# Batch 0 of a fused Fourier mixing and ELU block: mirrored rows read forward and turned by flip products, loads and products by rows, and one list of operations

## The chip, the cores and the metric

The kernel runs on one core of a Trainium2 chip. The metric is the device time of one execution in microseconds (us). Three executions of the kernel before took 1909.07, 1910.53 and 1910.87 us; their median is 1910.53. A further execution was taken with the hardware profiler.

## What is computed

The reference takes x of shape (8, 3008, 256) in float32, applies a Fourier transform along the sequence and one along the channels, keeps the real part, and passes every row through two matrix products with an ELU between them:

```python
X = np.fft.fft(x, axis=1)
X = np.fft.fft(X, axis=2)
x = X.real.astype(np.float32).reshape(8 * 3008, 256)
h = x @ w_in                                   # (256, 2048)
g = np.where(h > 0.0, h, np.exp(np.minimum(h, 0.0)) - 1.0)
return (g @ w_out).astype(np.float32)          # (2048, 256)
```

w_in and w_out arrive as float64. The kernel takes them as pairs of 32-bit words and converts them itself.

## The kernel before

**The transform by mirrors.** The real part of a two-dimensional transform of real data needs only sums and differences of mirrored entries. The kernel folds the sequence twice and the channels once, so that a batch becomes small stationary matrices, which are multiplied with cosine and sine matrices. Four tiles xl0 to xl3 (L[0] to L[3]) hold the rows of a batch: L[0] the rows from 0 upward, L[1] those from the end of the batch downward, L[3] those from the middle (HALF = 1504) upward, L[2] those from the middle downward. Each has 128 partitions and six rows (m = 0 to 5) of 256 channels in the free dimension: four rows from the first 512, two from the next 256. Partition p holds rows 4p to 4p+3 of the one part and 2p, 2p+1 of the other. In the mirrored tiles the same partition must hold the mirrored rows, so partition p needs rows further back as p grows. The function load_x gets these (back, L248) by gathers on GpSimd's queue with a table of row numbers; the other two tiles come by plain loads (ahead, L262) on SyncE's queue (SP).

**Folds of batch 0.** fold_x (L683) makes of each tile a sum e and a difference o of mirrored channels, 128x768 each, and then sums and differences of the four e and the four o: the stationaries EO for the real part (e) and the imaginary part (o), of even and odd frequencies. All of it is on VectorE. fold_first (L894) does the same for channel 128 alone, which feeds a transform of its own ("x").

**Transforms.** A Dft (L952) multiplies its six stationary blocks (one for each m) with slices of MC, a matrix of 128x1887 per kind (R, I for real and imaginary, even and odd frequencies; O and J are the odd ones). dft_parts (L909) says which: the products with m = 1, 3, 5 ("odd") go to one PSUM bank, those with m = 0, 2, 4 ("even") to another. copy, unfold ("sum"), plus ("up") and minus ("down") make of the two banks the columns of a ring of 2048 columns in SBUF: Rr for the real, Ir for the imaginary part, and Rb for channel 128.

**Weights.** w_in and w_out come in eight chunks each (Chunk, L367; w0 to w7 and u0 to u7 in the list of names). A chunk is loaded raw (512 KB), and then converted by integer steps on VectorE (top, mantissa, sign: letters a, b, s), ScalarE (power, low, high: p, l, d) and GpSimd (round, multiply, pair: R, M, P). The w_in chunks are folded too: fold_chunk (f) multiplies a chunk with CC on TensorE into a PSUM bank, put_half (Ws, Wc) copies it into Wsc on ScalarE. The last row of Ws has to stand as a column in wex: for chunks 0 and 1 turn_last_row (wm, L651) does it by tiny products with "pick" on TensorE and put_last_row (wex, L662) copies them; for chunks 2 to 7 spread_last_row (L639) writes it to DRAM and reads it back by two DMAs.

**The second stage.** The columns of the ring are taken 256 at a time. A step is one w_in chunk of one such tile: P (mm_P, L1322) and Q (mm_Q, L1327) make h in a bank "H"; V (even_part, L1331) adds channel 128 on VectorE between them; h_minus, below (b), exp (x) and g follow on VectorE and ScalarE; Xa and Xb (mm_plain) multiply with w_out in the first two tiles, and mm_X1 to mm_X3 in all later ones. These first two tiles go in turns, so slot 0 is chunk 0 of tile 0 and slot 1 is chunk 0 of tile 1. A step of a later tile takes 4.8 us, which is PERIOD (T in the code).

**The order.** Everything is put into a list of events with a time, and emitted in the order of these times; operations wrapped in pin keep this order on their engine, so each engine works through a queue that is written out by hand. The DMA loads are not wrapped. FRONT (L1747) is the part of the list for batch 0 and the first slots, written as lines of names with a time. Loads that the front needs are issued ahead of it (L1643 to L1651) or by load_rest (L1670), which waits for the gathers by way of a one-element copy into MC (L1673). In front of all that stand 46 products of zeros on TensorE (L1640), which write a bank that nobody reads. Later batches (1 by mirror_folds on GpSimd, 2 to 7 by quarters) have other code and are not touched.

Of the kernel before, what the change touches and what calls it, by code (L numbers as in the profile page):

```python
# [36 lines left out]
BS = 4  # L37

# [135 lines left out]

@with_exitstack
def kernel(
# [16 lines left out]
    CC_dr = nc.inline_tensor(_chan_consts(), name="chan_mats")  # L193
    PK_dr = nc.inline_tensor(_pick_consts(), name="pick_mats")
# [46 lines left out]
    def load_x(b):  # L241

        L = [
            spool.tile([128, 6 * ND], FP, tag=f"xl{j}", bufs=1, name=f"xl{j}")
            for j in range(4)
        ]

        def back(j, few):  # L248
            cols = slice(0, 2 * ND) if few else slice(2 * ND, 6 * ND)
            c = 1 if few else 0  # L250
            pin(
                nc.gpsimd.indirect_dma_start(
                    out=L[j][:, cols],
                    out_offset=None,
                    in_=xflat,
                    in_offset=bass.IndirectOffsetOnAxis(
                        ap=ix[:, c : c + 1].bitcast(U32), axis=0
                    ),
                    element_offset=(b * SEQ + (HALF if j == 1 else 0)) * ND,
                )  # L260
            )
        def ahead(j, row):  # L262
            nc.sync.dma_start(out=L[j][:, 0 : 4 * ND], in_=xrows(b, row, 4, 128, 4))
            nc.sync.dma_start(
                out=L[j][:, 4 * ND :], in_=xrows(b, row + 512, 2, 128, 2)
            )

        loads = [lambda n=n: back(2 - n // 2, n % 2) for n in range(4)]
        return L, loads + [lambda: ahead(3, HALF), lambda: ahead(0, 0)]
# [278 lines left out]
    def load_mats(ri, kodd, cuts=()):  # L548
        n = (2 * ri + kodd) * BW
        ends = (0, *cuts, BW)  # L550
        for a, z in zip(ends, ends[1:]):
            nc.sync.dma_start(
                out=MC[ri, kodd][:, a:z], in_=MC_dr.ap()[:, n + a : n + z]
            )
# [128 lines left out]
    def fold_x(L, engine_of, cuts_of):  # L683

        ops = {}

        def op(key, o, a, b, f):
            tt = lambda o, a, b, f: pin(
                engine_of(key).tensor_tensor(out=o, in0=a, in1=b, op=f)  # L689
            )  # L690
            cuts = cuts_of(key, o.shape[1])
            for i in range(len(cuts) - 1):
                c = slice(cuts[i], cuts[i + 1])
                ops[key, i] = lambda c=c: tt(o[:, c], a[:, c], b[:, c], f)

        E, O = [], []
        for j in range(4):
            e = spool.tile([128, 6 * 128], FP, tag=f"e{j}", bufs=1, name=f"e{j}")
            o = spool.tile([128, 6 * 128], FP, tag=f"o{j}", bufs=1, name=f"o{j}")
            ev, ov = (  # L700
                t.rearrange("p (m o d) -> p m o d", o=2, d=64) for t in (e, o)
            )
            src = L[j].rearrange("p (m d) -> p m d", d=ND)
            if j in (1, 2):
                src = src[:, ::-1]

            lo, hi = (
                t.rearrange("p m (d o) -> p m o d", o=2)
                for t in (src[:, :, 1:129], src[:, :, 255:127:-1])
            )  # L710
            op(f"e{j}", ev, lo[:, :, ::-1], hi[:, :, ::-1], ALU.add)
            ops[f"c{j}", 0] = lambda e=ev[:, :, 0, 63:64], s=src[:, :, 0:1], j=j: (
                act(e, s)
                if engine_of("c") is nc.vector and j != 1
                else pin(engine_of("c").tensor_copy(out=e, in_=s))
            )
            op(f"o{j}", ov, lo, hi, ALU.subtract)
            E.append(e)
            O.append(o)
        ops["x1", 0] = lambda: act(L[1][0:1, 5 * ND :], L[0][0:1, 0:ND])  # L720
        op("E0", E[0], E[0], E[1], ALU.add)
        op("E2", E[2], E[2], E[3], ALU.add)
        op("EO0", E[1], E[0], E[2], ALU.add)
        op("EO1", E[3], E[0], E[2], ALU.subtract)
        op("O0", O[0], O[0], O[1], ALU.subtract)
        op("O2", O[2], O[2], O[3], ALU.subtract)
        op("EO2", O[1], O[0], O[2], ALU.subtract)
        op("EO3", O[3], O[0], O[2], ALU.add)
        return [E[1], E[3], O[1], O[3]], ops
# [164 lines left out]
    def fold_first(L):  # L894

        c = [t.rearrange("p (m d) -> p m d", d=ND)[:, :, 128:129] for t in L]
        c[1], c[2] = c[1][:, ::-1], c[2][:, ::-1]
        a = spool.tile([128, 6], FP, tag="xa", bufs=1, name="xa")
        g = spool.tile([128, 6], FP, tag="xg", bufs=1, name="xg")
        vtt(a.unsqueeze(2), c[0], c[1], ALU.add)  # L900
        vtt(g.unsqueeze(2), c[2], c[3], ALU.add)
        d = state["x_odd"] = spool.tile([128, 6], FP, tag="xd", bufs=1, name="xd")
        vtt(d, a, g, ALU.subtract)
        e = spool.tile([128, 6], FP, tag="xe0", bufs=1, name="xe0")
        vtt(e, a, g, ALU.add)
        return e


# [9 lines left out]
    def dft_mms(ps, ri, kodd, par, stat, width):  # L918
        for j, (m, c, n, o) in enumerate(dft_parts(ri, kodd, par)):
            mm(  # L920
# [31 lines left out]
    class Dft:  # L952
# [7 lines left out]
        def mms(self, par, ps):  # L960
            dft_mms(ps, self.ri, self.kodd, par, self.stat, 1 if self.first else 128)
# [678 lines left out]
    for _ in range(46):  # L1640
        mm(idle, zero, zero[:, 0:1].to_broadcast([128, 512]), True)
    exp_neg(warm)
    L_first, loads = load_x(0)  # L1643
    for load in loads[:5]:
        load()
    w1_chunks[0].load()
    loads[5]()
    nc.sync.dma_start(out=CC, in_=CC_dr.ap())
    load_mats(0, 0, (BE,))
    w1_chunks[1].load()  # L1650
    nc.sync.dma_start(out=pick, in_=PK_dr.ap())  # L1651
    EO, ops = fold_x(
        L_first,
        lambda key: nc.vector,
        lambda key, n: (0, 4, n) if key in ("e0", "e2") else (0, n),
    )

    def dft_now(d, par, tag):
        d.mms(par, bank(tag))

    R_even, I_even = Dft(0, 0, 0, EO[0]), Dft(1, 0, 0, EO[2])
    R_odd, I_odd = Dft(0, 0, 1, EO[1]), Dft(1, 0, 1, EO[3])
# [7 lines left out]
    def load_rest():  # L1670

        ops["x1", 0]()
        act(MC[1, 0][0:1, 0:1], L_first[1][0:1, 0:1])  # L1673
        load_mats(1, 0)
        w2_chunks[0].load()
        w1_chunks[2].load()
        load_mats(0, 1)
        for chunk in (w1_chunks[3], w2_chunks[1], w1_chunks[4], w2_chunks[2]):
            chunk.load()
        load_mats(1, 1)  # L1680
        w1_chunks[5].load()
        w2_chunks[5].load()

    def open_x(b):
        state["L"], state["loads"] = load_x(b)

    def begin_x_even():
        state["x_even"] = Dft(0, 0, 0, fold_first(L_first), ring=Rb, first=True)

    def copy_row(cols):  # L1690
# [9 lines left out]
        ("xs", begin_x_even),  # L1700
        ("xl1", load_rest),
# [4 lines left out]
    for (key, i) in list(ops):  # L1706
        names[key + "ab"[i] if key in ("e0", "e2") else key] = ops[key, i]
    for c in range(6):
        for name, chunk in ((f"w{c}", w1_chunks[c]), (f"u{c}", w2_chunks[c])):
            for key, fn in zip(  # L1710
                "abpldRsMP",
                (chunk.top, chunk.mantissa, chunk.power, chunk.low, chunk.high,
# [7 lines left out]
        names[f"wex{c}"] = lambda c=c: put_last_row(c)  # L1720
    for k, d, tags in (
        ("x", lambda: state["x_even"], ("pC", "pD")),
        ("R", lambda: R_even, ("pA", "pB")),
        ("I", lambda: I_even, ("pC", "M")),
        ("O", lambda: R_odd, ("pA", "pB")),
        ("J", lambda: I_odd, ("H", "H")),
    ):
        names[f"{k}-even"] = lambda d=d, tags=tags: dft_now(d(), 0, tags[0])
        names[f"{k}-odd"] = lambda d=d, tags=tags: dft_now(d(), 1, tags[1])
        names[f"{k}-copy"] = lambda d=d: d().copy()  # L1730
        names[f"{k}-sum"] = lambda d=d: d().unfold()
        names[f"{k}-up"] = lambda d=d: d().plus()
        names[f"{k}-down"] = lambda d=d: d().minus()
    names["L"] = lambda: [open_x(1)] + [state["loads"][n]() for n in (4, 5)]
    for n in range(4):
        names[f"L{n}"] = lambda n=n: state["loads"][n]()
    for slot in range(8):
# [9 lines left out]
    FRONT = (  # L1747
        (-20.84, "e3 o3"),
        (-19.11, "w0a w0b w0p w0R c3"),
        (-17.62, "w0s w0M"),  # L1750
        (-16.21, "e0a e2b o2"),
        (-14.32, "e2a o0 c2"),
        (-12.89, "E2 f0 O2"),
        (-11.63, "xl1 xs e1 x-even"),
        (-9.8, "e0b c1 o1 c0 x-odd x-copy Wc0"),
        (-8.58, "E0 Ws0 EO0"),
        (-7.29, "wm0 wex0 O0 R-odd"),
        (-5.76, "w1b EO2"),
        (-4.55, "w2b R-even u0b w2d u0a EO1 w1d"),
        (-3.25, "I-odd R-copy w1l w1a x-sum u0l"),  # L1760
# [348 lines left out]
```

## Time and profile before

| | |
|---|---|
| runs | 1909.07, 1910.53, 1910.87 us; median 1910.53 |
| profiled execution | 1909.52 us |
| its span, first to last instruction | 1907.7 us |
| granted TensorE clock over the span | 1.00 |
| TensorE busy | 1899.9 us |
| VectorE, GpSimd, ScalarE busy | 1466.4, 1348.9, 877.1 us |
| moved by DMA | 73.80 MB, of it 16.03 MB in the first 45 us |

The page lists each engine's busy time and its share of the span. "PE" is TensorE's products and "PEld" its weight loads, which overlap them. A product in float32 is made of two instructions, so the counts in rows of products are twice those in the code. In rows of the timeline there stand start, length, engine, line of the code, operation, what is written and read, shape, count, and in brackets the idle time of the engine before it with what ended it. Nearly all operations have the line of a helper (L592 all products, L598 most of VectorE's, L604 ScalarE, L601 GpSimd), so they are told apart by tile and shape. "SPq" is SyncE's queue, where a row is the issue of a DMA and not its transfer. In stretches of time, each row gives start and end, length, busy time and count of each engine, then the granted clock, the mean busy share of the sixteen DMA engines and the GB/s that they moved.

### The profile page before, as it was taken

To read this page: it belongs to the slowest core of one execution; us is meant where nothing else is said; L and a number is where in the kernel's file an instruction comes from. 1 tells how busy PE (TensorE), PEld (TensorE's weight loads), DVE (VectorE), ACT (ScalarE), POOL (GpSimd) and SP (SyncE) were. 2 spreads that over 40 slices of the span, in tenths; PEclk is the share of its full clock that TensorE was granted. 3 is DMA by queue.
4 is the path that set the end of the run, shared out by engine and by line. 5 is a ranking of instruction groups with operands and counts; after the bars stand their busy time and mean duration, and the time that the engine had idled before them with its cause. 6 is when DMAs were issued, how large, how long until landed. Compare 5 with 4: busy or idle time off the path is not lost.

```text
span 1907.7 us, 27911 instructions
## 1 busy us (share of the span) xinstructions
PE 1899.9 (100%) x8972; PEld 1649.8 (86%) x8972; DVE 1466.4 (77%) x2788; ACT 877.1 (46%) x1711; POOL 1348.9 (71%) x1834
## 2 busy tenths in 40 slices
PE   9999999999999999999999999999999999999999
PEld 6888888888888888888888888888888888888887
DVE  8766667887878878778777787877878778777666
ACT  5754444444444444444444444444444444444443
POOL 4887667786677766777667777687766777556664
PEclk9999999999999999999999999999999999999999
DMA  8145211211011110111112111022110210100101
GB/s 339 45 33 43 57 24 45 52 24 36 12 44 41 32 33 12 46 40 30 31 19 49 34 28 30 13 56 44 24 24 16 55 20 16 17 12 15 20 12 23
DMA packets 278934, 73.80 MB, mean 39 GB/s; under 512 B 254402, under 2 KB 268998, under 8 KB 278788
## 3 DMA queue, kind: packets, MB, share of 16 engines
q1 hardware_dynamic: 270148, 61.58, 15.9%
q0 software_dynamic: 6464, 10.18, 1.7%
q8 instruction: 71, 1.16, 0.3%
q14 instruction: 75, 0.61, 0.1%
q10 hardware_dynamic: 2176, 0.26, 0.1%
HBM read 47.10 MB, written 24.80 MB: 38 GB/s over the span
## 4 chain that ended last, share of the span: by engine, by line
PE 97%; DVE 2%; DMA 0%; issue 0%; ACT 0%; POOL 0%; ACTq 0%; POOLq 0%; DVEq 0%
PE H L592 38%; PE pB L592 17%; PE pC L592 17%; PE pD L592 17%; PE pA L592 9%; DMA xl<-in_x_dram,ix 0%; DVE e L689 0%; DVE o L689 0%; POOL w L601 0%; DVE E L1339 0%; DVE pow L460 0%; DVE w L418 0%; DVE v L598 0%; DVE u L598 0%; ACT Wsc L604 0%
## 5 line engine op out<-in xcount | busy, mean ns | idle before, releaser
L601 POOL TENSOR_TENSOR G<-G 128x256 f32<-128x256 f32 x1437 | 1045.8, 737 | 504.1 <-DVE G L1369 346.9
L604 ACT ACTIVATE G<-H 128x512 f32<-128x512 f32 x376 | 224.4, 597 | 929.1 <-DVE G L1353 925.5
L1339 DVE SCALAR_TENSOR_TENSOR E<-Rb,wex,H 128x256 f32<-128x256 f32 x752 | 327.6, 477 | 334.3 <-PE H L592 327.6
L592 PE MATMUL H<-Rr,Wsc 128*128 128x256 f32 x1504 | 387.7, 380 | 0.5 <-ACT Wsc L604 0.5
L592 PE MATMUL H<-Ir,Wsc 128*128 128x256 f32 x1504 | 386.8, 380 | 1.0 <-DVE E L1339 1.0
L592 PE MATMUL pC<-G,WT 128*128 128x256 f32 x1440 | 369.6, 379 | 0.0
L592 PEld LDWEIGHTS H<-Ir,Wsc 128*128 128x128 f32 x1504 | 278.4, 189 | 48.9 <-DVE E L1339 3.4
L592 PEld LDWEIGHTS H<-Rr,Wsc 128*128 128x128 f32 x1504 | 282.1, 190 | 41.6 <-issue 2.3
L592 PEld LDWEIGHTS pC<-G,WT 128*128 128x128 f32 x1440 | 273.6, 190 | 37.2
L1353 DVE SCALAR_TENSOR_TENSOR G<-E,H 128x512 f32<-128x512 f32 x376 | 256.9, 683 | 45.1 <-POOL G L601 11.5
L1369 DVE SCALAR_TENSOR_TENSOR G<-G,H 128x512 f32<-128x512 f32 x376 | 255.8, 680 | 39.6 <-ACT G L604 39.5
L1369 DVE SCALAR_TENSOR_TENSOR G<-M,G 128x512 f32<-128x512 f32 x376 | 256.6, 682 | 0.7 <-ACT M L604 0.7
L604 ACT ACTIVATE G<-G 128x512 f32<-128x512 f32 x376 | 233.4, 621 | 0.0
L592 PE MATMUL pA<-G,w 128*128 128x256 f32 x784 | 229.4, 379 | 0.0
L592 PE MATMUL pB<-G,w 128*128 128x256 f32 x784 | 229.4, 379 | 0.0
L592 PE MATMUL pD<-G,w 128*128 128x256 f32 x784 | 229.3, 379 | 0.0
L604 ACT ACTIVATE M<-G 128x512 f32<-128x512 f32 x376 | 224.2, 596 | 2.8 <-DVE G L1353 1.5
L604 ACT ACTIVATE M<-M 128x512 f32<-128x512 f32 x376 | 221.1, 588 | 0.1
L592 PE MATMUL pB<-G,WT 128*128 128x256 f32 x720 | 214.4, 379 | 0.0
L592 PE MATMUL pD<-G,WT 128*128 128x256 f32 x720 | 214.2, 379 | 0.0
L592 PEld LDWEIGHTS pA<-G,w 128*128 128x128 f32 x784 | 148.9, 190 | 20.7 <-DVE G L1369 0.3
L592 PEld LDWEIGHTS pB<-G,w 128*128 128x128 f32 x784 | 148.9, 190 | 20.4 <-PE H L592 0.2
(172 smaller groups left out, 1555.3 us busy)
## 6 DMA issues: line engine op xcount, KB each, us to landing
out_dram<-ot SPq DMA_DIRECT2D x496, 32.0 KB
xq<-in_x_dram SPq DMA_DIRECT2D x48, 94.0 KB
out_dram<-ot SPq DMA_DIRECT2D x256, 2.0 KB
Rb<-r SPq DMA_DIRECT2D x10, 376.0 KB
raw<-in_moe_w_in_dram SPq DMA_DIRECT2D x7, 512.0 KB
MC<-dft_mats SPq DMA_DIRECT2D x3, 943.5 KB
xq<-in_x_dram SPq DMA_DIRECT2D x12, 192.0 KB
xq<-in_x_dram SPq DMA_DIRECT2D x36, 64.0 KB
```

The lines of the kernel that those rows point to most:

```text
L592: nc.tensor.matmul(out_, lhsT=lhsT, rhs=rhs, start=start, stop=stop, skip_group_check=True)
L601: pin(nc.gpsimd.tensor_tensor(out=o, in0=a, in1=b, op=op))
L604: pin(nc.scalar.activation(out=o, in_=i, func=func, **kw))
L1339: nc.vector.scalar_tensor_tensor(out=S.E[:, c], in0=Rb[:, cols(i)], scalar=wex[:, f : f + 1], in1=S.H[:, c], op0=ALU.mult, op1=ALU.add,)
L1353: nc.vector.scalar_tensor_tensor(out=two(S.G[:, 0:512])[:, :, ::-1], in0=two(S.E), scalar=2.0, in1=two(S.H), op0=ALU.mult, op1=ALU.subtract,)
L1369: nc.vector.scalar_tensor_tensor(out=o, in0=e, scalar=-1.0, in1=h, op0=ALU.add, op1=ALU.max)
```

## The change

**Loads of batch 0.** load_first replaces the gathers of four rows per partition for L[1] and L[2] by plain loads on SP: the rows are read forward, so they stand in the wrong partitions. L[2] takes 128 partitions of four rows. L[1] would need row 3008 in its last place, so it takes 127 partitions from SP, and three rows and one row for partition 127 by two small DMAs from ScalarE's queue. The gathers of two rows per partition stay. ahead is split in two.

**Flip products.** Four products with flip, a 128x128 matrix of ones on the counter-diagonal (64 KB, loaded too), turn the partitions of these rows into banks "H", two rows of 256 channels each (turn). mirror adds a turned pair of rows to its partner in L[0] or L[3], with the channels reversed; rows 4 and 5, which were gathered, are added from SBUF.

**Folds by rows.** first_folds replaces fold_x and fold_first. Rows are taken in three groups: a (m = 1, 3), b (m = 0, 2), c (m = 4, 5). After the mirrored sums, add makes the sums of L[0] and L[3] (Z) on VectorE, GpSimd their differences (Zd, Ze), and only these two are folded over the channels (e, o; em, om for the odd frequencies, om on GpSimd). The products of the first transforms follow the groups: "1" means the first two blocks of a bank, "2" the third. MC of R is loaded in four pieces.

**One list.** FRONT is now one list without times, ahead of all other events, and holds the loads of x, matrices and chunks too (x, m, and the letter g). 13 zero products stand at the start, and the names d3 and d8 put 3 and 8 more behind the four flip products. P2 and P3 stand ahead of Xa0.

**Elsewhere.** The steps of the chunks outside the list move from -0.5, 0.05 and 0.06 to 0.95, 0.96 and 0.97 in their slot, which is behind V at 0.9. The last rows of chunks 6 and 7 are turned by TensorE.

The diff, cut to its core:

```diff
+WARM = 13
...
+def _flip_consts():
+
+    return np.eye(128, dtype=np.float32)[::-1].copy()
...
+    def load_first(L, j, few):
+
+        if few or j in (0, 3):
+            L_loads[j, few]()
+            return
+        n = 128 if j == 2 else 127
+        row = (HALF if j == 2 else SEQ) - 511
+        nc.sync.dma_start(out=L[j][0:n, 2 * ND :], in_=xrows(0, row, 4, n, 4))
+        if j == 1:
+            for c, r, m in ((2, SEQ - 3, 3), (5, 0, 1)):
+                nc.scalar.dma_start(
+                    out=L[j][127:128, c * ND : (c + m) * ND],
+                    in_=xrows(0, r, 4, 1, m),
+                )
+
+    def first_folds(L):
+
+        flip = spool.tile([128, 384], FP, tag="side", bufs=2, name="flip")[:, 0:128]
+        rows = [t.rearrange("p (m d) -> p m d", d=ND) for t in L]
+        plus, minus = rows[1][:, ::-1], rows[2]
...
+        def turn(j, m):
+            ps = turned[j, m.start] = bank("H").rearrange("p (m d) -> p m d", d=ND)
+            mm(ps, flip, rows[(1, 2)[j == 3]][:, ::-1][:, m], True)
+
+        def mirror(j, m):
+            own = rows[j]
+            if m is rest:
+                other = rows[(1, 2)[j == 3]][:, ::-1][:, m]
+            else:
+                other = turned[j, m.start]
+            vtt(own[:, m, 1:], own[:, m, 1:], other[:, :, :0:-1], ALU.add)
+            vtt(own[:, m, 0:1], own[:, m, 0:1], other[:, :, 0:1], ALU.add)
...
+        def add(m):
+            vtt(plus[:, m], rows[0][:, m], rows[3][:, m], ALU.add)
+
+        def even(m):
+            fold(0, 0, m, vtt)
+            edge(0, m, vcopy)
+
+        near, odd, even_, rest = slice(0, 4), slice(1, 4, 2), slice(0, 3, 2), slice(4, 6)
+        every = slice(0, 6)
+        for key, m in (("a", odd), ("b", even_), ("c", rest)):
+            for j in (0, 3):
+                if m is not rest:
+                    ops[f"t{j}{key}"] = lambda j=j, m=m: turn(j, m)
+                ops[f"y{j}{key}"] = lambda j=j, m=m: mirror(j, m)
+            ops["Z" + key] = lambda m=m: add(m)
+            ops["e" + key] = lambda m=m: even(m)
+        ops["oab"] = lambda: fold(0, 1, near, vtt)
+        ops["oc"] = lambda: fold(0, 1, rest, vtt)
+        for key, c in (("Zd", slice(0, 3 * ND)), ("Ze", slice(3 * ND, 6 * ND))):
+            ops[key] = lambda c=c: gtt(L[2][:, c], L[0][:, c], L[3][:, c], ALU.subtract)
+        ops["em"] = lambda: fold(1, 0, every, vtt)
+        ops["cm"] = lambda: edge(1, every, act)
+        ops["om"] = lambda: fold(1, 1, every, gtt)
+        ops["fl"] = lambda: nc.sync.dma_start(out=flip, in_=FL_dr.ap())
...
-    def dft_mms(ps, ri, kodd, par, stat, width):
+    def dft_mms(ps, ri, kodd, par, stat, width, some=range(3)):
...
-    for _ in range(46):
-        mm(idle, zero, zero[:, 0:1].to_broadcast([128, 512]), True)
+
+    def keep_warm(n):
+        for _ in range(n):
+            mm(idle, zero, zero[:, 0:1].to_broadcast([128, 512]), True)
+
+    keep_warm(WARM)
...
+        ("m0a", lambda: load_mats(0, 0, BE, BE + 2 * NE)),
+        ("m0b", lambda: load_mats(0, 0, 0, 2 * NH)),
+        ("m0c", lambda: load_mats(0, 0, 2 * NH, BE)),
+        ("m0d", lambda: load_mats(0, 0, BE + 2 * NE)),
...
-    FRONT = (
-        (-20.84, "e3 o3"),
...
+    FRONT = """
+        x2a x3a fl t3b x1a x0a t3a x3b x0b m0c m0a m0b m0d w0g cc m1 y3a pk w1g t0a
+        x1b m2 t0b x2b y3b y0a w2g y3c y0c Za d3 d8 x-odd1 y0b ea R-odd1 Zb eb Zc
+        w0a w0p ec w0b x-even1 R-even1 oab x-even2 w0R w0s w5g R-even2 R-odd2 oc w0M
+        R-copy I-odd f0 u0g u1g w1b x-copy w1d Ze u5g Ws0 R-sum w1a x-odd2 w1l Zd
+        w1R I-even x-sum Wc0 I-copy u2g u3g wm0 em R-up m3 w2b x-up wex0 P0 Irc
+        x-down I-sum cm O-even w2l R-down Irc2 w1p I-up V0 R4 w4g Q0 w1s w3g P1 om
+        u0b w2d u0a u0d w1M h0 w1P O-copy O-odd u0l V1 f1 I-down b+0 u0p x+0 b-0 Ws1
+        u0R Wc1 x-0 w2a Q1 g+0 u0s wm1 wex1 h1 g-0 u2l b+1 w2p u1l xd P2 u0M b-1 x-1
...
+    """.split()
...
-        for dt, fns in zip((-0.5, 0.05, 0.06, 2.95), chunk.steps()):
+        for dt, fns in zip((0.95, 0.96, 0.97, 2.95), chunk.steps()):
...
-    for c, t in ((2, 15.2435), (3, 23.1265)) + tuple((c, (2 * c - 1) * T + 0.04) for c in range(4, 8)):
-        at(t, lambda c=c: spread_last_row(c))
+    for c in range(4, 6):
+        at((2 * c - 1) * T + 0.04, lambda c=c: spread_last_row(c))
+    for c in range(6, 8):
+        at((2 * c - 1) * T + 3.02, lambda c=c: turn_last_row(c))
+        at((2 * c - 1) * T + 3.03, lambda c=c: put_last_row(c))
```

## The prediction

> **What bounds the kernel now.** I read the page first: TensorE is busy over the whole span, so only two things can move the time: the moment at which useful products begin, and the waits and extra products after that.
>
> ```profile
> span 1907.7 us, 27911 instructions
> PE 1899.9 (100%) x8972; PEld 1649.8 (86%) x8972; DVE 1466.4 (77%) x2788; ACT 877.1 (46%) x1711; POOL 1348.9 (71%) x1834
> ```
>
> Second, the timeline of the first 102 us, TensorE's rows and one weight-load row. The dummy products on "zero" are not work. The weight loads show when the clock rises: until 6.64 they come every 0.43 us, afterwards 32 of them fit in 6.85, which is 0.21 each.
>
> ```profile
> 1.14 12.85 PE L592 MATMUL M<-zero 128*128 128x512 bf16 x46 [1.14 <-DVE zero L579]
> 6.64 6.85 PEld L592 LDWEIGHTS <-zero 128*128 128x128 bf16 x32 [0.25 <-issue]
> ...
> 13.82 1.89 PE L592 MATMUL H<-w,CC 128*128 128x256 f32 x8
> 16.36 1.54 PE L592 MATMUL pC<-MC,xe 128*128 128x189 f32 x6 [0.65 <-DVE xe L598]
> 17.75 2.06 PE L592 MATMUL pD<-MC,xe 128*128 128x377 f32 x6
> 19.65 0.50 PE L592 MATMUL H<-pick,Wsc 128*128 128x1 f32 x4
> 20.37 2.17 PE L592 MATMUL pB<-MC,e 128*128 128x377 f32 x6 [0.22 <-DVE e L689]
> ...
> 26.84 1.02 PE L592 MATMUL H<-Rr,Wsc 128*128 128x256 f32 x4
> ...
> 35.24 0.61 PE L592 MATMUL H<-pick,Wsc 128*128 128x1 f32 x4 [0.61 <-ACT Wsc L604]
> 35.71 1.11 PE L592 MATMUL H<-Rr,Wsc 128*128 128x256 f32 x4
> ...
> 60.21 1.13 PE L592 MATMUL H<-Rr,Wsc 128*128 128x256 f32 x4 [0.54 <-ACT Wsc L604]
> ...
> 101.58 1.13 PE L592 MATMUL H<-Ir,Wsc 128*128 128x256 f32 x4 [0.69 <-DVE E L1339]
> ```
>
> From 20.37 the stream is closed except for a few waits of 0.5 to 0.7. My marker is 26.84, where the first product of the second stage (P0) starts: all that is before it is front, and what is after it hardly changes.
>
> Third, the chain of waits up to the marker: a gather of x, then VectorE's folds one behind the other.
>
> ```profile
> 3.18 8.17 DMA xl<-in_x_dram,ix
> 11.80 0.87 DVE o L689
> 13.27 0.87 DVE o L689
> 14.92 0.95 DVE o L689
> 16.31 1.21 DVE e L689 x2
> ```
>
> Fourth, the transfers, as stretches of time (the last two columns are the DMA share and GB/s).
>
> ```profile
> 8.00:40.00 32.00, 30.52 (x132) 21.03 (x131) 30.41 (x62) 16.88 (x37) 10.80 (x11) 1.00 1.03 409
> 164.10:166.60 2.50, 2.50 (x13) 2.15 (x13) 0.87 (x2) 1.35 (x4) 2.34 (x4) 1.00 0.29 47
> 313.92:314.20 0.28, 0.28 (x3) 0.25 (x2) 0.00 (x0) 0.28 (x2) 0.21 (x1) 1.00 0.09 14
> ```
>
> From 8 to 40 us sixteen engines move 409 GB/s, 25.6 each. In the second stretch one load of 94 rows is under way (L334, 94 KB, whose DRAM side is 2 times 47 rows) and moves at some 47: two engines' worth. In the third a store of 31 rows (L1574, 3.9 KB) goes at 14 GB/s and a share of 0.09: one engine's worth.
>
> **What the Trainium skill says.** "DMA: Bandwidth & Descriptors", section "Why a DMA increments its semaphore by 16 and not by 1": a copy is split over the largest number of engines up to 16 that divides the slowest dimension of both sides; it names 127 partitions as a case of one engine. The two small stretches agree (94 against 2: two; 31: one); no transfer of 127 rows is in this trace. Same page, "Queues, rings and completion order": on each engine a queue's descriptors are taken in order, and different queues take turns. The views don't separate engines, so no row shows it. "TensorE: Matmul & The Clock Gate", section "What's actually happening": an idle window of about 3.4 us halves the clock, a busy one restores it. The rise at 6.64 agrees; the fall isn't shown, as TensorE's longest gap before is 0.65.
>
> **The change part by part.** (1) *Loads.* The two big gathers go. Rows of x2 and x3 come by 128-row loads. The mirrored rows of x1 come as one SP load of **127 rows** of 4 KB plus two scraps on ACT's queue. By the rule above the 127-row load runs on one engine: 127 x 4096 = 520,192 bytes at 25.6 GB/s = **20.3 us**. It is fourth in SP's queue, so on that engine 8 packets of x2, 8 of x3 and the flip table lie ahead. Bytes in the first stretches reach 0.58 MB at 4.0 and 1.1 MB at 5.2, so it begins at 5.2. The two small gathers left take turns with it there, 32 KB, 1.3. It ends at 26.8 by this sum; I take 26.5, as one engine alone should gain a little. From last byte to use I allow 0.6 (x3's 786 KB were through at 4.6, its first fold began at 5.25). x1 is usable at **27.1**. Spread over 16 engines it would be at 9.3: 1.63 MB lie up to its end in SP's queue and 0.52 MB in the two gathers, and the stretches have moved 2.15 MB by 8.6.
>
> All that SP issues behind it, SP's order kept, has a sixteenth of its bytes on the same engine: 1.28 us for 512 KB, 0.64 for 256, 0.47 for 189, 2.35 for a 943 KB matrix. Ends plus 0.6: x0's four rows 28.4, x3's two 29.0, x0's two 29.7, the odd matrix part (MC00, 377 KB) 31.1, w1 chunk 0 33.3, second matrix 36.1, w1 chunk 1 37.4. Without the queue they would be 17 to 18 earlier.
>
> (2) *Flip products.* Four, each 512 columns in f32: 0.86 warm (the x4 group of 256 columns at 30.85 is followed by the next at 31.71), 1.7 cold. The two on x2 run at 6.7 to 8.4, right behind the 13 dummies, hidden. The first on x1, t0a, waits until 27.1 with all of TensorE's list behind it: every product. TensorE idles from 8.4 to 27.1, the clock falls: 1.7 + 1.7, to 30.5. Then 11 dummies, "d3 d8": cold till 5.5 after 27.1 as at the start (1.14 to 6.64), so five at 0.43 and six at 0.21: **33.9**. Bounds: no fall, 31.2 (then the adds decide); cold throughout, 35.2.
>
> (3) *Folds.* VectorE had four e and four o folds of 0.88 and eight sums of 0.88 to 0.95; it gets six mirror pairs, three sums and folds by rows. Prices: 512 elements 0.61 behind another (12.58 to 13.18), 256 0.34, a scrap 0.09; so a mirror pair is 0.70, a two-row fold with edge 0.44. y0a starts when t0a is out, 29.0; y3c to 30.4, y0c to 31.1, Za to 31.7, all under the dummies. The rest (y0b, ea, Zb, eb, Zc, ec, oab, oc, with chunk 0's four steps between) ends at 38.4 and is each time 0.3 to 2 ahead of its product. The two 768 differences and the om fold on POOL, about 1.9 each by its 1.29 for 512, begin when L0 and L3 are summed and are wanted 10 us later: nothing. If POOL were late, O-even would pay, under 1 us.
>
> (4) *Products up to P0*, warm: x-odd1 1.27, R-odd1 1.27, five pieces of 0.64, I-odd 1.90, f0 1.73, x-odd2 0.64, I-even 1.28, wm0 0.25: 11.5. P0 at 33.9 + 11.5 = **45.4**, against 26.84: **+18.6**.
>
> (5) *From P0 to P2.* Before 8.87 (26.84 to 35.71), with the wait for the second half of Ws1. The new order has the same products. I find waits of 0.35 (O-even for the edge copy behind ACT's row copies), 0.4 (f1 for POOL's pair) and 0.8 (Ws1, Wc1): 8.95. **+0.1**.
>
> (6) *Later waits.* At 60.21 Wc3 stood behind ACT's b+; it now stands well ahead of it in the list. At 101.58 the V step was queued on VectorE behind a chunk's integer step, now put behind V (0.95). At 113.04 wex arrived by DMA. With 0.17 pipeline each: 0.7 + 0.9 + 0.1. I give back 0.5 for new ones that I can't see: **-1.2**. Chunks 6 and 7 turn their last row by products: 0.47 each by 35.24 to 35.71: **+0.9**. The bank they hold is free before the third P behind them. The chunk loads moved into the list are behind x1 too, but their uses are shifted as much.
>
> Sum: 18.6 + 0.1 - 1.2 + 0.9 = **+18.4** on the profiled execution's 1909.52 (span 1907.7 and 1.8 around it), 1927.9. The median of the runs is 1910.53, 1.0 higher: 1928.9. I say 1928.8.
>
> **Rivals.** *The 127 rows are spread like 128* (slower turns to not slower): x1 usable at 9.3, then x0's last rows at 11.95 bind; y0c, Za to 13.4, products from 13.5, P0 at 25.0: -1.8 + 0.1 - 1.2 + 0.9 = -2.0, so 1908.5. For it: the rows are contiguous in DRAM and could be cut otherwise. Against it: 94 and 31 rows weren't. It decides from about 12 engines on; at 8 engines the load takes 2.5 and the gain is gone. *The late load starves what is behind it*: weights and matrices come so late on the slow engine that f1, O-even or chunk 2 wait anew, 2 to 5 more: 1933. Against it: by (1) they keep their distance. *The clock doesn't fall*: 2.7 less, 1926; TensorE's idle stretch of 18.7 speaks against it.
>
> **How the numbers follow.** One engine for x1: 0.85 (of it 0.10 starved, 0.08 no fall). Spread: 0.15, of which 0.05 gains over 3.8. Beyond 0.2%, 3.8 us, a change can be told from none. Ends in the likely case: 1928.8 - 2.7 (no fall) - 1.4 (engine at 27.5 GB/s, a sixteenth of the best stretch's 440, 18 to 19 us) - 0.5 (no new waits) = 1924; upward 1.4 (cold) + 1.3 (at 24 GB/s, as the 94 rows) + 3 (starving) = 1934.5. To leave no more than 0.2 out I widen to 1922 to 1936. Slower 0.85, same 0.10, faster 0.05.
>
> **What would show it.** DMA near 26 GB/s, one engine's worth, from about 12 to 27 us; the third flip product at 27; P0 at 45; the same spacing as before from 70 us on; no row at 101 waiting for E. A third flip product near 9.5 and P0 at 25 would prove me wrong at step (1).

## The result, and the profile after

| | before | after |
|---|---|---|
| median, runs of one comparison | 1909.80 us (1908.83 to 1910.87, 4 runs) | 1931.53 us (1931.12 to 1932.27, 4 runs) |
| ratio of the times, 95% interval | | 1.0114 [1.0097, 1.0132] |
| profiled execution | 1909.52 us | 1932.27 us |
| its span | 1907.7 us | 1930.5 us |

The kernel after is slower by 1.14%. 1928.8 was forecast, in a range of 1922 to 1936.

The page of the kernel after, its span and first section: TensorE is busy nearly as long as before, so the span has grown by a pause.

```profile
span 1930.5 us, 27900 instructions
PE 1902.0 (99%) x8966; PEld 1650.3 (85%) x8966; DVE 1465.3 (76%) x2789; ACT 878.0 (45%) x1710; POOL 1352.9 (70%) x1835
```

TensorE's timeline of the kernel after. The second row on "flip" holds the third and fourth flip product, which turn rows of x1; behind it come the zero products and the first transforms. 48.80 is P0, the marker of the prediction, and 58.85 is P2.

```profile
6.57 1.88 PE L603 MATMUL H<-xl,flip 128*128 128x512 f32 x4
29.49 3.75 PE L603 MATMUL H<-xl,flip 128*128 128x512 f32 x4 [21.04 <-DMA xl<-in_x_dram]
33.03 2.93 PE L603 MATMUL M<-zero 128*128 128x512 bf16 x11
35.80 1.43 PE L603 MATMUL pD<-MC,xl 128*128 128x377 f32 x4
37.96 1.53 PE L603 MATMUL pB<-MC,e 128*128 128x377 f32 x4 [0.73 <-DVE e L758]
...
48.80 1.11 PE L603 MATMUL H<-Rr,Wsc 128*128 128x256 f32 x4
...
55.58 1.13 PE L603 MATMUL H<-raw,CC 128*128 128x256 f32 x4 [0.44 <-POOL raw L612]
...
58.38 0.60 PE L603 MATMUL H<-pick,Wsc 128*128 128x1 f32 x4 [0.81 <-ACT Wsc L615]
58.85 1.97 PE L603 MATMUL H<-Rr,Wsc 128*128 128x256 f32 x8
```

One bracket holds the result: TensorE stands for 21.04 us until rows of x have landed. P0 starts 21.96 later than before's 26.84, P2 23.14 later than its 35.71. From P2 to the end the kernel before takes 1871.99 and the kernel after 1871.65. All the loss lies in front of P2.

The same pause in stretches of time (before the last three columns the busy time and count of PE, PEld, DVE, ACT, POOL):

```profile
7.00:12.00 5.00, 1.45 (x4) 0.38 (x2) 1.42 (x4) 0.00 (x0) 0.00 (x0) 1.00 0.06 26
12.00:14.00 2.00, 0.00 (x0) 0.00 (x0) 0.00 (x0) 0.00 (x0) 0.00 (x0) 0.83 0.06 27
14.00:26.00 12.00, 0.00 (x0) 0.00 (x0) 0.00 (x0) 0.00 (x0) 0.00 (x0) 0.50 0.59 179
26.00:29.00 3.00, 0.00 (x0) 0.00 (x0) 0.00 (x0) 0.00 (x0) 0.00 (x0) 0.50 0.07 27
```

A share of 0.06 to 0.07 of sixteen engines is one engine, at 26 to 27 GB/s. It is alone until 14 us and again from 26 on; in between other engines carry loads that stand behind x1. The granted clock begins to fall between 12 and 14 us and is 0.50 from 14 on.

SyncE's queue shows what the long transfer does to the loads behind it. The first row is x1's 127 rows, the second the first four rows of x0.

```profile
2.22 0.33 SPq L701 DMA_DIRECT2D xl<-in_x_dram  x1
2.60 11.38 SPq L276 DMA_DIRECT2D xl<-in_x_dram  x1
14.02 2.44 SPq L272 DMA_DIRECT2D xl<-in_x_dram  x2
16.50 7.94 SPq L565 DMA_DIRECT2D MC<-dft_mats  x4
29.37 0.39 SPq L403 DMA_DIRECT2D raw<-in_moe_w_in_dram  x1
```

The issue of x0's load lasts 11.38 us, where the rows ahead of it take 0.3 to 0.5. It waits for no semaphore (the counter by which a load tells that its bytes have landed); that its packets found no room behind x1's on the one engine is an inference. w1's first chunk is issued at 29.37, when x1 has landed: its load counts up the same semaphore as x1's and waits for it.

Last, VectorE and GpSimd at the start of the folds, which the prediction had at no cost:

```profile
34.85 1.37 DVE L609 TENSOR_TENSOR e<-xl 128x256 f32<-128x256 f32 x1
36.25 1.65 DVE L758 COPY e<-xl 128x2 f32<-128x2 f32 x1
37.82 0.68 DVE L609 TENSOR_TENSOR xl<-xl,xl 128x512 f32<-128x512 f32 x1
38.53 0.43 DVE L609 TENSOR_TENSOR e<-xl 128x256 f32<-128x256 f32 x1
38.99 0.17 DVE L758 COPY e<-xl 128x2 f32<-128x2 f32 x1
```

```profile
33.81 4.07 POOL L612 TENSOR_TENSOR xl<-xl,xl 128x768 f32<-128x768 f32 x2 [29.68 <-DMA CC<-chan_mats]
```

The same fold takes 1.37 us in the first row and 0.43 in the fourth, the same copy 1.65 and 0.17. The slow pair lies inside GpSimd's two differences (33.81 to 37.88); the copy of two elements ends when the second difference does.

### The profile page after: what moved, and what is told of

Same layout as the page of the kernel before. It is cut to its first block, busy times and chain, and to the rows that moved or that the text cites. A ratio compares the mean times of both kernels' runs of the same rounds, so it can differ in the third digit from the quotient of the medians.

```text
span 1930.5 us, 27900 instructions
## 1 busy us (share of the span) xinstructions
PE 1902.0 (99%) x8966; PEld 1650.3 (85%) x8966; DVE 1465.3 (76%) x2789; ACT 878.0 (45%) x1710; POOL 1352.9 (70%) x1835
## 4 chain that ended last, share of the span: by engine, by line
PE 96%; DVE 1%; DMA 1%; ACT 1%; SPq 1%; issue 0%; POOL 0%; ACTq 0%; DVEq 0%; POOLq 0%
PE H L603 37%; PE pB L603 17%; PE pC L603 17%; PE pD L603 17%; PE pA L603 9%; DMA xl<-in_x_dram 1%; SPq L276 1%; ACT G L615 0%; ACT Wsc L615 0%; DVE xl L609 0%; ACT pow L615 0%; POOL w L612 0%; DVE v L609 0%; PE M L603 0%; DVE pow L475 0%
## 5 line engine op out<-in xcount | busy, mean ns | idle before, releaser
L1403 DVE SCALAR_TENSOR_TENSOR G<-E,H 128x512 f32<-128x512 f32 x376 | 257.2, 684 | 41.7 <-POOL G L612 11.5
```

Of the source, the lines that this page charges most:

```text
L1403: nc.vector.scalar_tensor_tensor(out=two(S.G[:, 0:512])[:, :, ::-1], in0=two(S.E), scalar=2.0, in1=two(S.H), op0=ALU.mult, op1=ALU.subtract,)
```

## The experiments

Each ratio compares with the kernel before on the same chip, which had medians of 1909.39 (with e1 to e4), 1909.26 (e5 to e8), 1909.59 (e9, e10) and 1909.42 (e11, e12). Times of the kernel after are those of the table, from a comparison of its own. Of e2, e3, e4, e6, e7 and e8 there is one execution each, the profiled one.

**e1: x1 in 112 + 15 rows.** The same bytes in two loads; 112 divides by 16 and 15 by 15.

```diff
-        nc.sync.dma_start(out=L[j][0:n, 2 * ND :], in_=xrows(0, row, 4, n, 4))
+        for a, z in ((0, n),) if j == 2 else ((0, 112), (112, n)):
+            nc.sync.dma_start(
+                out=L[j][a:z, 2 * ND :], in_=xrows(0, row + 4 * a, 4, z - a, 4)
+            )
```

> The 127-row load of x1 is cut into 112 and 15 rows; nothing else differs from the changed kernel. Theory (the 127 rows ran on one DMA engine, because 127 is prime): 112 rows go over 16 engines and 15 over 15, x1 is usable near 9.3 us, the third flip product starts there and not at 29.5, P0 near 25 to 26 instead of 48.8, and the time is about 1908.5 us, 23 less than the changed kernel's 1931.5 and 1 to 2 under the kernel before. Rival (the flip products, the dummies or the new list are what costs): P0 stays above 40 and the time above 1925.

Measured: 1913.58 us, ratio to before 1.0022 [1.0014, 1.0030]. TensorE's timeline of e1:

```profile
10.34 1.96 PE L603 MATMUL H<-xl,flip 128*128 128x512 f32 x4 [1.63 <-DMA xl<-in_x_dram]
12.13 2.56 PE L603 MATMUL M<-zero 128*128 128x512 bf16 x11
14.71 1.51 PE L603 MATMUL pD<-MC,xl 128*128 128x377 f32 x4
18.28 1.53 PE L603 MATMUL pB<-MC,e 128*128 128x377 f32 x4 [2.07 <-DVE e L761]
...
29.12 1.11 PE L603 MATMUL H<-Rr,Wsc 128*128 128x256 f32 x4
```

The third flip product comes 19.2 us earlier than in the kernel after, and the time falls by 18.0 us through the cut of the load alone. In the trace of the kernel after the semaphore of the 127 rows is raised at the end of the issue and then only once, at 29.36; here that of the 112 rows is raised sixteen times from 7.06 to 10.02, and that of the 15 rows fifteen times from 7.74 to 10.21. 4.2 us of loss to the kernel before are left, and P0 comes at 29.12, not at 25 to 26: that needs another cause. The 2.07 in front of R-odd1 is the first candidate. R-odd1 waits for e, which VectorE's folds make.

**e2: the kernel before, with one load cut badly.** The first rows of x3, 128 in one load, become 127 + 1.

```diff
-            nc.sync.dma_start(out=L[j][:, 0 : 4 * ND], in_=xrows(b, row, 4, 128, 4))
+            for a, z in ((0, 127), (127, 128)) if b == 0 and j == 3 else ((0, 128),):
+                nc.sync.dma_start(
+                    out=L[j][a:z, 0 : 4 * ND],
+                    in_=xrows(b, row + 4 * a, 4, z - a, 4),
+                )
```

> The kernel before, with its first load (four rows per partition of x3, 128 partitions) cut into 127 rows and 1 row; flip products, list and folds are those of before. Theory of one engine: the first fold waits until about 22 to 24 us instead of 5.25, the first product of the second stage moves from 26.8 to 43 to 46, and the time is 1926 to 1930 us. Rival (the form of the load is not what costs): within 2 us of 1910.

Measured: 1934.03 us. VectorE's first fold, at 5.25 in the kernel before:

```profile
30.40 0.96 DVE L693 TENSOR_TENSOR e<-xl 128x768 f32<-128x768 f32 x1 [29.32 <-DMA xl<-in_x_dram]
```

P0 starts at 50.93, and 24.6 us are lost to before: the mechanism shows without any other part of the change. The size is beyond what was expected, because the fold starts at 30.40 and not at 22 to 24. The 127 rows landed at 29.50 and the two rows per partition of x3 behind them at 30.27; on the way, packets of the four gathers took turns with them until 15.5. The folds and products behind pass 24.1 of the fold's 25.2 us on to P0.

**e3: 122 + 5 rows.** As e1, but 122 is 2 times 61, so two engines carry it.

```diff
-        for a, z in ((0, n),) if j == 2 else ((0, 112), (112, n)):
+        for a, z in ((0, n),) if j == 2 else ((0, 122), (122, n)):
```

> The changed kernel with x1's load cut into 122 and 5 rows. By the rule of the largest divisor up to 16, 122 is 2 times 61, so two engines, 10.2 us: x1 usable near 16.5, the third flip product there, P0 near 32 to 34, the time near 1915 us. Rival (only the odd or prime count matters, any even count is spread): as with 112 and 15 rows, 1908.5. Second rival (any count other than 128 or 96 goes to one engine): as the changed kernel, 1931.

Measured: 1922.55 us, 9.0 above e1, where the kernel after is 18.0 above it; P0, at 39.12, is 10.0 behind e1's, the kernel after's 19.7. A stretch of e3, two engines' worth:

```profile
14.00:20.00 6.00, 0.17 (x1) 0.20 (x2) 0.00 (x0) 0.00 (x0) 0.00 (x0) 0.50 0.14 57
```

The loss over e1 halves with the second engine, and the semaphore of the 122 rows is raised twice behind the issue (18.43 and 19.51). This ties the loss to the number of engines, not to rows being forward or flipped. The size was missed: the third flip product came at 19.82 and not at 16.5, and the time is 7.5 above the 1915 expected. Neither rival fits (1908.5 or 1931).

**e4: the clock kept up.** The kernel after with 96 more zero products ahead of the third flip product.

```diff
-        ... w1g t0a
+        ... w1g d96 t0a
```

> The changed kernel, 127 rows as they are, with 96 more products of zeros (21 us at full clock) ahead of the third flip product, so that TensorE is not idle while it waits. If the clock's fall costs what I say: the two flip products take 1.7 instead of 3.4 us, the 11 dummies 2.4 instead of 2.9, P0 moves from 48.8 to about 46.5, the time is 2 to 3 us less, near 1929. Rival (the adds on VectorE and the late loads behind x1 decide anyway): P0 moves by less than 0.7 us.

Measured: 1930.78 us. TensorE's timeline of e4:

```profile
28.65 1.93 PE L603 MATMUL H<-xl,flip 128*128 128x512 f32 x4
30.42 2.56 PE L603 MATMUL M<-zero 128*128 128x512 bf16 x11
32.82 1.43 PE L603 MATMUL pD<-MC,xl 128*128 128x377 f32 x4
36.19 1.54 PE L603 MATMUL pB<-MC,e 128*128 128x377 f32 x4 [1.95 <-DVE e L758]
```

Of the 2.98 that x-odd1 gains, 0.84 is x1 being there earlier in this execution and 2.14 the clock. At R-odd1 1.77 is left: the wait for e has grown from 0.73 to 1.95. P0, at 47.03, keeps the 1.77. Less the 0.84, the fallen clock costs about 1 us, between what was expected and the rival, and VectorE hides the rest of it.

**e5: GpSimd's differences on VectorE.** e1 with Zd and Ze moved.

```diff
-            ops[key] = lambda c=c: gtt(L[2][:, c], L[0][:, c], L[3][:, c], ALU.subtract)
+            ops[key] = lambda c=c: vtt(L[2][:, c], L[0][:, c], L[3][:, c], ALU.subtract)
```

> The kernel after with x1's rows cut into 112 + 15 (as in e1_rows_112_15), and the two differences Zd and Ze on VectorE instead of GpSimd. Theory (while GpSimd works through a 768-element difference, VectorE's fold of two SBUF inputs and its small copy stand until the GpSimd instruction ends): with no GpSimd work there, the first 256-element fold takes 0.42 and the edge copy 0.17, R-odd1 waits under 0.3 for e instead of 2.07, and P0 comes at 27.2 to 28.3 (29.12 in e1; 1.8 gained, up to 1 lost to the 1.8 us of differences now in VectorE's queue ahead of the folds of I and of em). O-even may wait up to 1 for em. Time 1911.5 to 1913. Rival (the fold is slow by itself, by its strided reads or by the transfers of that time): fold 1.37 and copy 1.65 again, P0 at 29 or, with VectorE fuller, at 30; time 1913.5 to 1915.

Measured: 1910.81 us, ratio to before 1.0010 [1.0003, 1.0017]. VectorE's timeline of e5 at the same fold and copy, and at the integer step of a chunk later on:

```profile
14.46 0.42 DVE L609 TENSOR_TENSOR e<-xl 128x256 f32<-128x256 f32 x1
14.91 0.17 DVE L761 COPY e<-xl 128x2 f32<-128x2 f32 x1
14.99 0.69 DVE L609 TENSOR_TENSOR xl<-xl,xl 128x512 f32<-128x512 f32 x1
...
25.57 1.06 DVE L433 TENSOR_SCALAR w<-raw 128x512 int32<-128x512 int32 x1
```

The fold takes 0.42 and the copy 0.17, with the same operands. R-odd1 doesn't wait; P0 starts at 26.06, 3.06 earlier than in e1 and 0.78 earlier than in the kernel before. Part of the 3.06 is x1 landing earlier here (third flip product 9.62 against 10.34). The rival, a fold slow by itself, is out. What is left of the loss lies behind P0: P2 comes at 36.81, 1.10 behind the 35.71 of the kernel before, with waits of 0.76 at O-even, 0.35 at Q0 and 0.80 at wm1. The integer step at 25.57, 0.42 elsewhere, is held in turn, by GpSimd's rounding of the next chunk (25.00, 1.34).

**e6: the edge copies on ScalarE.** e1 with `edge(0, m, act)` in place of `edge(0, m, vcopy)`.

> As e1_rows_112_15, but the 2-element edge copies of the e folds are done by ScalarE. GpSimd keeps its two differences from 14.1 to 18.2. Theory A (only a VectorE copy is held up by GpSimd): the sum Zb (512 elements, two SBUF inputs) starts at 16.6 right behind the fold and takes 0.68; R-odd1 starts near 17.0 (18.28 in e1), P0 near 28.0. Theory B (every VectorE instruction with two SBUF inputs is held up too): Zb starts at 16.6 but lasts till GpSimd's second difference ends at 18.2, some 1.7 to 2.0 long; R-odd1 near 17.0, but R-odd2 or x-even1 waits behind Zb instead, and P0 comes at 28.0 to 29. The fold itself stays at 1.37 by both.

Measured: 1911.83 us. VectorE and GpSimd in e6:

```profile
14.78 1.37 DVE L609 TENSOR_TENSOR e<-xl 128x256 f32<-128x256 f32 x1
16.18 2.18 DVE L609 TENSOR_TENSOR xl<-xl,xl 128x512 f32<-128x512 f32 x1
18.40 0.43 DVE L609 TENSOR_TENSOR e<-xl 128x256 f32<-128x256 f32 x1
18.74 0.69 DVE L609 TENSOR_TENSOR xl<-xl,xl 128x512 f32<-128x512 f32 x1
```

```profile
13.74 4.07 POOL L612 TENSOR_TENSOR xl<-xl,xl 128x768 f32<-128x768 f32 x2 [9.60 <-DVE xl L609]
```

Theory B: with the copy gone, the sum Zb (0.69 when free) is held for 2.18 in its place. R-odd1 comes at 16.44 and P0 at 28.30. Instructions with two inputs in SBUF are held as the copy is, while mirror sums with one input in PSUM beside the same difference (14.12, two in 0.74) are not.

**e7: the old offsets of the chunk steps.** e1 with (-0.5, 0.05, 0.06, 2.95) again.

> As e1_rows_112_15, but the integer steps of the chunks outside the list stand again at -0.5, 0.05 and 0.06 in their slot. By step (6) of the prediction the wait of P or Q for E behind such a step comes back: one or more waits of 0.5 to 0.9 for E between 50 and 110 us, and the stretch from P2 to the end is 0.7 to 1.5 longer than in e1_rows_112_15; time 1913 to 1915. Rival (the new offsets do nothing, and what the stretch gained came from the order of the list): no such row, and the stretch from P2 to the end is within 0.3 of e1's.

Measured: 1915.07 us. From P2 (40.76) to the end (1913.3) it takes 1872.54; e1 takes 1871.54 (1910.7 less 39.16). Two products of e7:

```profile
106.81 1.13 PE L603 MATMUL H<-Ir,Wsc 128*128 128x256 f32 x4 [0.29 <-DVE E L1392]
...
114.11 0.61 PE L603 MATMUL H<-pick,Wsc 128*128 128x1 f32 x4
```

Counted from P2, the first comes 0.45 later than in e1, and the second another 0.39: it waits for Ws's copy on ScalarE, which ends at 114.05. The remaining 0.1 lies far behind. Both waits begin on VectorE: an integer step stands right ahead of E (105.01, 0.97), and the next one (107.87) takes 2.33 beside a GpSimd instruction, where e1's takes 0.67, so that ScalarE starts later on all that precedes the copy. So the new offsets are worth some 0.8 in this pair of executions. The front of e7 was 1.6 later than e1's, with products at the lower clock, and isn't compared.

**e8: x1 from ScalarE's queue.** The kernel after with `nc.scalar.dma_start` for the 127 rows.

> The kernel after with the load of x1's 127 rows issued from ScalarE's queue instead of SyncE's; it still runs on one engine. SyncE's queue is then not held behind it. Theory (what counts is only when x1 lands: its own bytes on one engine, 20 us): third flip product at 27 to 30, P0 at 47 to 50, although w1's first chunk is issued before 20 us instead of at 29.4. Rival (queues take turns on that engine, and the shares of the other loads, about 4 MB / 16 = 10 us, now stand between x1's packets): third flip product at 33 to 38, P0 at 52 to 57. If the held queue itself cost something (the other loads late), P0 would come 1 to 2 sooner after the flip product than in the kernel after, where it was 19.3.

Measured: 1933.18 us; third flip product at 29.52, P0 at 48.81, both within 0.03 of the kernel after. SyncE's queue in e8:

```profile
2.63 26.92 SPq L272 DMA_DIRECT2D xl<-in_x_dram  x2
29.59 1.85 SPq L565 DMA_DIRECT2D MC<-dft_mats  x4
```

What was expected of SyncE was wrong: it stood for 26.92, until x1 had landed, now because the second of these loads is given the semaphore that x1's load counts up (number 100 on both in the trace) and waits for it. That the first matrix parts were issued 13 us later than in the kernel after cost P0 nothing. For P0, only the landing of x1 counts.

**e9 and e10: further orders.** e9 is e5 with y3c ahead of y0a and y0c behind ea, 5 zero products instead of 11, and the edge copy cm on VectorE behind em. e10 adds to it: product and pair of w1's chunk 1 on VectorE, O-odd in two parts around f1, and DMAs again for the last rows of chunks 6 and 7.

```diff
-        ... y3b y0a w2g y3c y0c Za d3 d8 x-odd1 y0b ea R-odd1 Zb eb Zc
+        ... y3b y3c w2g y0a Za d5 x-odd1 y0b ea R-odd1 y0c Zb eb Zc
-        ops["cm"] = lambda: edge(1, every, act)
+        ops["cm"] = lambda: edge(1, every, vcopy)
```

> As e5_diff_on_vector, with three things reordered: the mirror pair y3c runs before y0a, in the stretch where VectorE waits for the flip product, and y0c behind ea; the 11 zero products become 5; the edge copy cm goes to VectorE right behind em. Theory (the front is bound by the chain flip product, mirror pair, sum, first product, and O-even by the edge copy behind ScalarE's row copies): x-odd1 at 12.6 (13.96 in e5), P0 at 24.7 to 25.4 (26.06), no wait of 0.76 at O-even, P2 at 34.4 to 35.6 (36.81); time 1909.0 to 1910.0. Rival (behind x-odd1 VectorE is the bound and TensorE waits for sums and folds instead): waits of 0.3 to 1 at R-odd1, x-even1 or R-even1, P0 at 26 or later, time as in e5, 1910.8.

> As e9_order; besides, the product and the pair of w1's chunk 1 are on VectorE instead of GpSimd, O-odd is split so that its last block runs between f1 and wm1, and the last rows of chunks 6 and 7 go by DMA again as in the kernel before. Theory: VectorE's integer step of 1.50 beside GpSimd's product falls back to 0.42, f1 doesn't wait, the wait of 0.80 at wm1 shrinks to 0 to 0.3; 0.36 is saved for each of the two chunks, less a wait of 0.1 near 110 us. P2 at 33.8 to 35.0, time 1907.5 to 1909.0, that is 0.3 to 1.8 below the kernel before. Rival (VectorE's queue gets 1.5 us more and h, b or g of the first slots come late): new waits at Q1, Xa0 or Xb0 of 0.5 to 1, time 1909 to 1910.5.

Measured: 1914.94 and 1915.84 us, ratios 1.0030 [1.0018, 1.0041] and 1.0030 [1.0018, 1.0043]; both theories missed. VectorE in e9, then GpSimd:

```profile
25.00 0.95 DVE L609 TENSOR_TENSOR e<-xl 128x768 f32<-128x768 f32 x1
25.98 1.14 DVE L761 COPY e<-xl 128x6 f32<-128x6 f32 x1
27.04 0.54 DVE L609 TENSOR_TENSOR Rr<-bs,pB 128x377 f32<-128x377 f32 x1
27.49 2.01 DVE L433 TENSOR_SCALAR w<-raw 128x512 int32<-128x512 int32 x1
```

```profile
25.20 1.90 POOL L612 TENSOR_TENSOR w<-raw,w 128x512 f32<-128x512 f32 x1 [21.07 <-ACT raw L615]
27.06 2.16 POOL L612 TENSOR_TENSOR o<-xl 128x768 f32<-128x768 f32 x1
```

The edit itself had put a VectorE copy beside GpSimd's rounding: a copy of six elements ends with it after 1.14, and the integer step behind it ends with om after 2.01. P0 waits 1.24 for the ring and Q0 2.74. The rounding is longer as well, 1.90 against 1.29 in e6: the fold em (first row) has begun before it and ends at 25.95. And y3c waited 2.19 for gathered rows, so that the sum Za came no sooner. In e10 the wait at wm1 fell to 0.47 as expected, but chunks 6 and 7 by DMA brought a wait of 1.77 for E at 118.11, where 0.1 was expected: VectorE stood 4.44 for wex to arrive by DMA.

**e11 and e12: the copy back on ScalarE.** Both are e5 with cm on ScalarE right behind em, and with e10's changes to chunk 1 and O-odd; e11 also has Za right behind y0a, y3c and y0c behind eb, and 5 zero products.

> As e5_diff_on_vector, with the edge copy cm kept on ScalarE but placed right behind em; product and pair of w1's chunk 1 on VectorE; O-odd split around f1; and the sum Za right behind y0a, the mirror pairs y3c and y0c behind eb, with 5 zero products instead of 11. Theory (VectorE must not copy beside a GpSimd instruction; O-even waits for cm only because of its place on ScalarE): no wait at O-even, f1 not late, wm1 waits 0.5 instead of 0.8; x-odd1 at 12.6 to 12.9, P0 at 25.2 to 25.6 (26.06 in e5), P2 at 34.8 to 35.6 (36.81); time 1908.6 to 1909.8. Rival (the third blocks, which now wait for Zc behind two mirror pairs, give the gain back): a wait of 0.6 to 1 at x-even2, P0 at 26 again, and P2 at 35.4 to 36: 1909.3 to 1910.2.

> As e11_best_2 without the last part (Za and the two mirror pairs stand as in e5, 11 zero products). Theory: P0 at 26.0 as in e5, no wait at O-even, P2 at 35.4 to 36.0; time 1909.3 to 1910.2, 0.6 to 1.5 below e5. If it's 1910.8 again, the waits removed have been replaced by others behind them.

Measured: 1911.04 and 1911.00 us, ratios 1.0008 [1.0000, 1.0016] and 1.0010 [1.0000, 1.0019]: no better than e5. In e11 O-even doesn't wait and wm1 waits 0.47, but Q0 has a wait of 1.72, since V0 comes on VectorE only at 30.06, behind the sums of the ring. In the profiled execution of e12, which is longer than its median, f1 waits 1.67 for chunk 1's pair, now on VectorE: the two halves took 1.84 beside a GpSimd instruction at 33.35, against 0.74 in e11. The waits have moved; VectorE sets the pace of this stretch. No version here beats the kernel before; the best ones stand within 0.2% of it, and 20.5 to 20.7 below the kernel after.

## Why the prediction was right, and where its sizes were off

**Step (1), one engine.** Right, and the cause of the loss: one engine's 26 to 27 GB/s; e1 takes 18.0 us away, e3 half of that, and e2 makes the loss in the kernel before. The rule of "DMA: Bandwidth & Descriptors" (section "Why a DMA increments its semaphore by 16 and not by 1") holds for 127, 122, 112 and 15 rows. x1's last packet ended at 28.95 and the flip product began at 29.49, where the sum had 26.5 and 27.1. The packets in the trace show which part was mis-sized. x1's first packet begins at 5.40 (5.2 in the sum), and until 10.1 eight packets of the gathers stand between x1's, 1.3 us as in the sum. While this engine works alone, up to 14 us, x1's packets of 4 KB follow one another every 0.155 us, which makes 19.7 for 127 (20.3 in the sum). But from 17 to 24, when other engines carry the loads behind x1, they follow every 0.19 to 0.20; from 14 to 24 that adds some 1.9. The first packet, which took 0.82, adds 0.7. The sum had one pace throughout. So the pace of one engine, the sign that the prediction named for 12 to 27 us, stands alone only up to 14 and from 26 on.

*Loads behind x1*: right in their distances, and 2.1 to 2.2 late, about as late as x1. x0's four rows landed at 30.57 (28.4 in the sum), x3's two at 31.20 (29.0), x0's two at 31.84 (29.7), the odd matrix part at 33.29 (31.1) and w1's first chunk at 35.51 (33.3). That cost P0 nothing, as e8 shows.

**Step (2), the clock.** Right: 0.50 from 14 us on. Two flip products took 3.54 (3.4 forecast), 11 zero products 2.77 (3.4). x-odd1 came at 35.80 instead of 33.9, which is step (1)'s 2.4 less 0.5. What the fall costs in the end is about 1 (e4), not the 2.7 of the rival "the clock doesn't fall", because the folds are next.

**Step (3), "each time 0.3 to 2 ahead of its product ... nothing".** This is the step whose mechanism failed. Differences on GpSimd were priced by when their results are wanted, and not by what they do to VectorE meanwhile. R-odd1 waited 0.73 for e (2.07 in e1). "SBUF — State Buffer", section "Who interferes with whom", says that a VectorE instruction with two SBUF inputs contends with a GpSimd instruction that reads SBUF, and so do copies and tensor_scalar in a two-port mode, and that the later one blocks fully. The traces agree: 1.37 for 0.42 and 1.65 for 0.17, and e5 and e6 show that it is GpSimd's work.

**Step (4), 11.5 to P0.** It took 13.00. 0.9 is that wait with the restart behind it, 0.2 a wider distance from wm0 to P0; some 0.35 is spread over the products.

**Step (5), 8.95 from P0 to P2.** It took 10.05. The three waits were there: 0.3 at O-even, 0.44 at f1, 0.81 at wm1. The sum of the step was wrong. The kernel before has one wait of 0.61 in its 8.87; 8.26 without it plus 1.55 is 9.8, and not 8.95. The order matters: before, O-odd stood behind f1 and Q1 and gave time for Ws1's copy; now it stands ahead of f1.

**Step (6), -0.3 net behind P2.** Right: 1871.99 became 1871.65, -0.34. No row near 101 waits for E. e7 finds some 0.8 of it in the offsets; each turned last row costs about 0.36 (0.47 in the sum).

The profiled sum is thus 2.4 - 0.5 + 1.5 + 1.1 = 4.5 more than forecast. Against the median it is 2.7, since this execution was 0.7 above its median and the forecast had put the median 1.0 above the execution. That the miss shrank on this way is luck. Steps (3) to (5) were 2.6 short, and the range held that only by terms meant for something else, a cold clock and starved loads.

## What to carry to other kernels

Count the rows of a load before its bytes: 127 rows on one engine cost 18 us that 112 + 15 don't, and every engine that waits for the list behind it pays. When a step is put on GpSimd because its result isn't wanted soon, look at what VectorE does in that time: copies, tensor_scalar steps and sums of two SBUF tiles stand until GpSimd is done, sums that read PSUM don't. An order that is packed this tightly gives a removed wait back at the next engine, so price the chain through VectorE before moving one of its steps.

## What was not expected of the hardware

A copy of 2 elements lasted 1.65 us and an integer step of 512 elements 2.01, each until GpSimd's instruction ended; free, they take 0.17 and 0.42. GpSimd is held in the same way when VectorE's instruction begins first: its rounding of 512 elements took 1.29 in e6, and 1.34, 1.59 and 1.90 in e5, e11 and e9, where the fold em, begun before it, still ran for 0.19, 0.43 and 0.75. One DMA engine's packets of 4 KB followed every 0.155 us while it worked alone, and every 0.19 to 0.20 beside busy engines. A load issued from another queue held SyncE for 26.92 us by way of a semaphore that both used.
